# Blocks of two units in one layout: 32 tokens of one sign side by side, for a Fourier mixing and SoLU kernel on one core

## The chip, the core and the metric

The kernel runs on one core of a Trainium2 chip. The core has a matrix engine (TensorE, PE in the profile, whose weight loads are listed apart as PEld), a vector engine (VectorE, DVE), an activation engine (ScalarE, ACT), a general engine (GpSimd, POOL) and a queue engine that issues most transfers (SyncE, SP). SBUF is the on-chip memory of 128 partitions, PSUM the matrix engine's result memory. The metric is the device time of one execution in microseconds (us), as the median of the runs.

## What is computed

Two stages follow each other. `x` is (8, 3136, 256), the weights are (256, 1024) and (1024, 256), all in float32:

```python
X = np.fft.fft(np.fft.fft(x, axis=1), axis=2).real      # (8, 3136, 256)
t = X.reshape(25088, 256)
h = t @ w_in                                            # (25088, 1024)
e = np.exp(h - h.max(-1, keepdims=True))
solu = h * e / (e.sum(-1, keepdims=True) + 1e-9)
mu = solu.mean(-1); var = ((solu - mu) ** 2).mean(-1)
out = ((solu - mu) / np.sqrt(var + 1e-6) * g_ln) @ w_out  # (25088, 256)
```

## The kernel before

**Units.** The sequence length 3136 is split as 49 x 64. The eight batch elements are taken as four pairs, and for each pair and each of 25 frequencies k1 there is one *unit* (class `Unit`, line 251): 128 tokens (2 batch elements x 64 values of k2) in the partitions. By the symmetry of a real transform one unit gives two results, the rows at k1 (sign 0) and the mirrored rows at 49 - k1 (sign 1); only k1 = 0 has one sign. So there are 100 units in a row, 96 of them with two signs.

**One iteration of the main loop** (from line 832) holds work of several units at once, written out by hand in the order in which each engine executes it (`tc.manual_schedule`):

- the *current* unit i: two products with the folded first weights on PE (`up`, line 259; eight matmuls of 512 columns), `even` and `join` on DVE, `expo` on ACT, `product` on DVE (u = h times exp), `square` on ACT, and at the end `turn_both` (line 334), a transpose on DVE in blocks of 32 x 32 from `both` (two signs x 1024 features) into the batch's tile `v`;
- the *previous* unit i - 1: `stats` (line 303), three small ACT instructions that make the variance `v` of each sign with a small term from the exponentials' sums, and `power` (line 313), one GpSimd instruction that raises it to -1/2, the factor `rs`;
- two units together, a *batch* (class `Batch`, line 318): in even iterations `move_blocks` (line 358) issues 16 transfers on SP that carry the 32 x 32 blocks of `v` to `uT`, where features are in the partitions, so that `uT` can be the stationary operand;
- the unit i - 4: `sums` (line 388), four additions or subtractions of 128 x 512 on GpSimd, which make the tiles S from the quarters of `uT`. The first waits for the DVE `product` of unit i - 1[...];
- the unit i - 5: the second product, `Down` (line 403). A unit's two signs of 128 tokens are a 2 x 2 block matrix A, and seven block products (`p1` to `p7`, each eight PE instructions on line 401, since a float32 product takes two) stand for eight, in the manner of Strassen and Winograd. `p1`, `p2` and `p4` have a quarter of `uT` as their stationary operand, the other four have a tile S. ACT (`keep_p`, `keep_x`, `keep_c`) and DVE (`finish`) scale the results with `rs` and join them in `ot`;
- the unit i - 6: `store` (line 475), sign 0 by SP in one transfer of 128 rows, sign 1 by an indirect transfer of GpSimd, whose row numbers are in `idx`.

About half of the iterations also carry a part of the next pair's Fourier stage (lines 109 to 215): loads on SP, additions on GpSimd and DVE, four matmuls on PE, one copy on ACT. The first five units take another way (`turn_whole`, line 341), through transposes on PE. In the last iterations no new units enter, the last batch is moved one unit at a time, and `sums` go to DVE.

**The layouts around the change.** In `v` the element order of a partition is (unit, feature, sign), so a transpose writes every second element:

```python
nc.vector.transpose(out=t.batch.v[:, t.w].rearrange("p f o -> p o f"), in_=t.both)
```

A transfer of `move_blocks` takes 32 partitions, with 16 runs of 64 elements in each (both signs of 32 tokens, alternating), 128 KB. In `uT` the tokens of the two signs therefore alternate as well, and `blocks` (line 379) gives the quarters with a step of two elements (8 bytes) between one stationary column and the next:

```python
uT = t.batch.uT[:, t.w].rearrange("p c i (n s) -> p s c (i n)", s=2)
return [uT[:, s, c : c + KF // 2] for s in range(2) for c in (0, KF // 2)]
```

The tiles S are written without gaps (128 columns in a row). The buffers: two `v`, two `uT`, one S for each unit of a batch, six `ot` for two signs of three units, seven of each small tile.

Of the kernel before, what the change touches and what calls it, by code (L numbers as in the profile page):

```python
# [9 lines left out]
FP32 = mybir.dt.float32  # L10
I32 = mybir.dt.int32
U32 = mybir.dt.uint32
ALU = mybir.AluOpType
# [4 lines left out]
P = 128  # L18


N1, N2 = 49, 64
NK = N1 // 2 + 1
# [4 lines left out]
NC = NH // CH  # L27
# [2 lines left out]


EVEN, ODD = slice(0, 129), slice(129, 256)


@with_exitstack
def kernel(
# [36 lines left out]
    small = ctx.enter_context(tc.tile_pool(name="small", bufs=7))  # L73
# [15 lines left out]
    idx = const.tile([P, NP * (NC + NK - 1)], I32, name="idx")  # L89
# [213 lines left out]
    def stats(t):  # L303

        n = slice(0, len(t.signs))
        es2, v = (small.tile([P, 2], FP32, tag=tag, name=tag) for tag in ("es2", "v"))
        nc.scalar.activation(out=es2[:, n], in_=t.esum[:, n], func=ACT.Square, bias=limits[:, 3:4], scale=1e-3)
        for s in t.signs:
            nc.scalar.activation(out=v[:, s : s + 1], in_=t.ssq[:, s : s + 1], func=ACT.Identity, bias=es2[:, s : s + 1],  # L309
                                 scale=float(FF) ** -3)  # L310
        t.v = v

    def power(t):
        n = slice(0, len(t.signs))
        t.rs = small.tile([P, 2], FP32, tag="rs", name="rs")
        nc.gpsimd.tensor_tensor(out=t.rs[:, n], in0=t.v[:, n], in1=neg_half[:, n], op=ALU.pow)  # L316

    class Batch:


        def __init__(self, by_blocks):
            if by_blocks:
                self.v = fpool.tile([P, 2, FF, 2], FP32, tag="v", name="v32", bufs=2)
            else:
                self.place()

        def place(self):
            self.uT = fpool.tile([P, 2, KF, 4, 64], FP32, tag="uT", name="uT", bufs=2)

    def turn_blocks(t, s):  # L330

        nc.vector.transpose(out=t.batch.v[:, t.w, :, s], in_=t.u[0 if len(t.signs) == 1 else s])

    def turn_both(t):
        if len(t.signs) == 2:
            nc.vector.transpose(out=t.batch.v[:, t.w].rearrange("p f o -> p o f"), in_=t.both)  # L336
        else:
            for s in range(2):
                turn_blocks(t, s)
# [17 lines left out]

    def move_blocks(batch, units, engines=(nc.sync,)):

        v = batch.v[:, units].rearrange("p w (c q n) s -> p q (w c) (n s)", q=4, n=32)  # L360
        uT = batch.uT[:, units].rearrange("p w c i m -> p i (w c) m")
        for i in range(4):
            for q in range(4):
                a, b = slice(32 * i, 32 * i + 32), slice(32 * q, 32 * q + 32)
                engines[i % len(engines)].dma_start(out=uT[b, i], in_=v[a, q])  # L365

# [10 lines left out]
            nc.gpsimd.tensor_tensor(out=Ws[:, j], in0=a, in1=b, op=ALU.subtract)  # L377

    def blocks(t):
        uT = t.batch.uT[:, t.w].rearrange("p c i (n s) -> p s c (i n)", s=2)  # L380
        return [uT[:, s, c : c + KF // 2] for s in range(2) for c in (0, KF // 2)]

# [20 lines left out]
    class Down:  # L403
# [6 lines left out]
        def __init__(self, t, fresh):  # L410
            self.t = t
            self.C11, self.X = (result(i)[:, 0:P] for i in (2, 3))
            self.S = blocks_of(t)
            self.PP = result(1)[:, 0 : 2 * P]
            self.P4, self.P5 = (self.PP[:, i * P : (i + 1) * P] for i in range(2))
            self.A11, self.A12, _, self.A22 = blocks(t)
            t.ot = [fpool.tile([P, D], FP32, tag="ot", name="ot", bufs=6) for _ in range(2)]
            if fresh:

                nc.tensor.matmul(self.X, ident, Wo[:, 0, 0:P], start=True, stop=True, skip_group_check=True)  # L420
# [11 lines left out]
            product7(self.P5, self.S[0], Ws[:, 0])  # L432

        def keep_p(self):
            nc.scalar.mul(out=self.t.ot[1], in_=self.PP, mul=self.t.rs[:, 1:2])  # L435

        def p2(self):
            product7(self.C11, self.A12, Wo[:, KF // 2 :, 0:P])
# [2 lines left out]
            product7(self.X, self.S[1], Ws[:, 1])  # L441

        def keep_x(self):
            nc.scalar.mul(out=self.t.ot[0][:, P:], in_=self.X, mul=self.t.rs[:, 0:1])  # L444

        def keep_c(self):
            nc.scalar.mul(out=self.t.ot[0][:, 0:P], in_=self.C11, mul=self.t.rs[:, 0:1])

        def p3(self):
            product7(self.P5, self.S[3], Wo[:, KF // 2 :, P:])  # L450
# [3 lines left out]

        def finish(self):
            o = self.t.ot[0][:, P:]
            nc.vector.scalar_tensor_tensor(out=o, in0=self.P5, scalar=self.t.rs[:, 0:1], in1=o, op0=ALU.mult, op1=ALU.add)
            o = self.t.ot[1].rearrange("p (i d) -> p i d", i=2)
            nc.vector.scalar_tensor_tensor(out=o, in0=self.X.unsqueeze(1).to_broadcast([P, 2, P]),
                                           scalar=self.t.rs[:, 1:2], in1=o, op0=ALU.mult, op1=ALU.add)  # L460

    def down(t, s, ps=None):

# [4 lines left out]
            nc.tensor.matmul(ps, uT[:, c, :, s], Wo[:, c, :], start=(c == 0), stop=(c == KF - 1))  # L468
        return ps

    def scale(t, s, ps):
        t.ot[s] = fpool.tile([P, D], FP32, tag="ot", name="ot", bufs=6)
        nc.scalar.mul(out=t.ot[s], in_=ps, mul=t.rs[:, s : s + 1])

    def store(t, s):

        if s:
            i = NP * NC + t.p * (NK - 1) + t.k1 - 1
            dma = nc.gpsimd.indirect_dma_start(  # L479
                out=out, out_offset=bass.IndirectOffsetOnAxis(ap=idx[:, i : i + 1], axis=0),  # L480
                in_=t.ot[s], in_offset=None)
        else:
            dma = nc.sync.dma_start(out=out_k[t.p, t.k1], in_=t.ot[s])

        tc.declare_no_dep(dma.ins, group=f"out{1 - s}", reason="other rows of the output")
        tc.add_to_no_dep_group(f"out{s}", dma.ins)

# [183 lines left out]
    with tc.manual_schedule():  # L671
# [77 lines left out]
            keep(first, c, slice(4 * KG, ZR))  # L749
        weights.load_table(1)  # L750
        lag = 5
        whole = 4

        def second_transform(i):
            if i < len(units):
# [4 lines left out]
        def enter(i):  # L760
            cur = units[i]
            if i % 2 == 0:
                batches.append(Batch(i >= whole))
            cur.batch, cur.w = batches[-1], i % 2

        def begin(i):
# [12 lines left out]
        batches = []  # L779
# [52 lines left out]
        for i in range(whole + 1, len(units) + lag + 1):  # L832
# [79 lines left out]
def _tables(B, S, D):  # L912

    import numpy as np

    def cs(num, den):
        a = 2.0 * math.pi * (num % den) / den
        return np.cos(a), np.sin(a)

    n1, k1 = np.arange(N1)[:, None], np.arange(NK)[None, :]  # L920
    c, s = cs(n1 * k1, N1)
    cm, sm = cs((n1 - N1 // 2) * k1, N1)
    zero = np.zeros_like(c)
# [19 lines left out]
    mirror = np.zeros((P, B // 2 * (NC + NK - 1)), np.int32)  # L943
    mirror[:PR, : B // 2 * NC] = load.transpose(1, 0, 2).reshape(PR, -1)
    rows = np.arange(B)[:, None, None] * S + (N1 - np.arange(1, NK)) + N1 * np.arange(N2)[::-1, None]
    mirror[:, B // 2 * NC :] = rows.reshape(B // 2, P, NK - 1).transpose(1, 0, 2).reshape(P, -1)
# [39 lines left out]
```

## Time and profile before

| | |
|---|---|
| runs | 1155.27, 1158.85, 1160.41 us; median 1158.85 us |
| the profiled execution | 1157.6 us, of which the span of the profiled instructions is 1155.8 us |
| granted PE clock | 0.998 of full speed |
| PE | 1109.1 us busy, 96% of the span |
| DVE | 1013.8 us, 88% |
| POOL | 848.0 us, 73% |
| ACT | 758.3 us, 66% |
| transfers | 185.75 MB in 458479 packets, 425750 of them under 512 bytes |

A group's row in the profile reads: line of the kernel, engine, operation, what is written <- what is read, size, count | busy time in us, mean duration in ns of one | idle time of the engine just ahead of it, and what ended that. A row of the timeline reads: start and length in us of a merged stretch, engine, line, operation, count, and in brackets the idle time ahead of it. Matmuls overlap, so the length of a stretch is more than the step from its start to the next one's; the steps between starts are what adds up to the time.

### The profile page before, as it was taken

To read this page: it belongs to the slowest core of one execution; us is meant where nothing else is said; L and a number is where in the kernel's file an instruction comes from. 1 tells how busy PE (TensorE), PEld (TensorE's weight loads), DVE (VectorE), ACT (ScalarE), POOL (GpSimd) and SP (SyncE) were. 2 spreads that over 40 slices of the span, in tenths; PEclk is the share of its full clock that TensorE was granted. 3 is DMA by queue.
4 is the path that set the end of the run, shared out by engine and by line. 5 is a ranking of instruction groups with operands and counts; after the bars stand their busy time and mean duration, and the time that the engine had idled before them with its cause. 6 is when DMAs were issued, how large, how long until landed. Compare 5 with 4: busy or idle time off the path is not lost.

```text
span 1155.8 us, 21664 instructions
## 1 busy us (share of the span) xinstructions
PE 1109.1 (96%) x7026; PEld 888.2 (77%) x7026; DVE 1013.8 (88%) x1440; ACT 758.3 (66%) x1725; POOL 848.0 (73%) x742
## 2 busy tenths in 40 slices
PE   2888999999999999999999999999999999999998
PEld 1555787888887778878887778878778788888887
DVE  7879988888999998888899998888898999898883
ACT  4567667666665766666666766666666676676661
POOL 3035888865898988866689888877499596777764
PEclk9999999999999999999999999999999999999999
DMA  9771798766998779866969697876697675865664
GB/s 238 204 192 39 168 191 195 184 145 145 160 187 160 180 177 184 198 138 143 164 139 204 150 189 171 203 175 141 149 159 146 137 163 122 150 144 111 139 135 111
DMA packets 458479, 185.75 MB, mean 161 GB/s; under 512 B 425750, under 2 KB 440350, under 8 KB 458368
## 3 DMA queue, kind: packets, MB, share of 16 engines
q1 hardware_dynamic: 444608, 146.22, 61.2%
q0 software_dynamic: 13760, 38.16, 12.4%
q8 instruction: 57, 0.93, 0.3%
q14 instruction: 54, 0.44, 0.1%
HBM read 44.78 MB, written 38.80 MB: 72 GB/s over the span
## 4 chain that ended last, share of the span: by engine, by line
PE 81%; DMA 5%; SPq 4%; DVE 4%; issue 2%; POOL 2%; ACT 1%; POOLq 0%; DVEq 0%; ACTq 0%
PE ps_m L401 48%; PE ps_h L264 25%; PE ps_m L208 4%; PE ps_m L236 3%; SPq L365 3%; DMA room<-in_x_dram 2%; DMA uT<-v 1%; DVE h L278 1%; POOL S L394 1%; DMA r<-q 1%; DVE u L293 1%; DMA F<-in_f_tab_dram 1%; SPq L216 1%; PE ps_m L468 1%; PE wps L601 1%
## 5 line engine op out<-in xcount | busy, mean ns | idle before, releaser
L264 PE MATMUL ps_h<-Wi,q 128*128 128x512 f32 x800 | 362.0, 594 | 7.9 <-DVE nmax L278 4.8
L394 POOL TENSOR_TENSOR S<-uT 128x512 f32<-128x512 f32 x186 | 251.1, 1350 | 104.6 <-DMA out_dram<-ot 40.9
L300 ACT ACTIVATE h<-u,usum 128x1024 f32<-128x1024 f32 x196 | 225.2, 1149 | 139.9 <-DVE u L293 139.9
L401 PE MATMUL ps_m<-Ws,S 128*128 128x128 f32 x2304 | 298.7, 276 | 4.3 <-issue 3.0
L401 PEld LDWEIGHTS ps_m<-Ws,S 128*128 128x128 f32 x2304 | 280.8, 192 | 8.8 <-issue 3.3
L264 PEld LDWEIGHTS ps_h<-Wi,q 128*128 128x128 f32 x800 | 144.0, 190 | 155.3 <-issue 139.9
L293 DVE SCALAR_TENSOR_TENSOR u<-h,u 128x1024 f32<-128x1024 f32 x196 | 259.4, 1359 | 0.8 <-ACT u L286 0.7
L286 ACT ACTIVATE u<-h,nmax 128x1024 f32<-128x1024 f32 x196 | 223.6, 1143 | 15.8 <-DVE nmax L278 11.8
L336 DVE STREAM_TRANSPOSE v<-u 128x2048 f32<-128x2048 f32 x93 | 215.5, 2317 | 3.2
L401 PE MATMUL ps_m<-Wo,uT 128*128 128x128 f32 x1536 | 213.1, 282 | 0.0
L401 PEld LDWEIGHTS ps_m<-Wo,uT 128*128 128x128 f32 x1536 | 197.3, 197 | 0.9 <-issue 0.9
L394 POOL TENSOR_TENSOR S<-uT,S 128x512 f32<-128x512 f32 x93 | 133.1, 1431 | 7.3
L278 DVE CUSTOM_DVE_ANT_0 h<-ev,ps_h 128x1024 f32<-128x1024 f32 x100 | 122.1, 1221 | 17.3 <-DVE ev L270 7.9
L479 POOL DMA_INDIRECT out_dram<-ot,idx x96 | 111.2, 1158 | 33.5 <-issue 16.6
L394 POOL TENSOR_TENSOR S<-S,uT 128x512 f32<-128x512 f32 x93 | 126.6, 1362 | 7.3
L278 DVE CUSTOM_DVE_ANT_0 h<-h,ps_h 128x1024 f32<-128x1024 f32 x96 | 117.3, 1221 | 14.2 <-ACT ot L444 0.5
L270 DVE SCALAR_TENSOR_TENSOR ev<-w_mid,r,ps_h 128x1024 f32<-128x1024 f32 x100 | 124.0, 1240 | 4.2 <-DMA r<-q 2.3
L401 PE MATMUL ps_m<-Ws,uT 128*128 128x128 f32 x768 | 106.2, 281 | 0.0
L401 PE MATMUL ps_m<-Wo,S 128*128 128x128 f32 x768 | 102.0, 276 | 0.7 <-ACT ot L435 0.7
L316 POOL TENSOR_TENSOR rs<-v,neg_half 128x2 f32<-128x2 f32 (+1 forms) x100 | 78.2, 782 | 28.4 <-ACT v L309 27.0
L236 PEld LDWEIGHTS ps_m<-T,g 128*128 128x128 f32 x400 | 60.1, 191 | 49.4 <-issue 45.8
L401 PEld LDWEIGHTS ps_m<-Ws,uT 128*128 128x128 f32 x768 | 98.0, 196 | 0.0
(96 smaller groups left out, 1135.5 us busy)
## 6 DMA issues: line engine op xcount, KB each, us to landing
uT<-v SPq DMA_DIRECT2D x752, 128.0 KB
out_dram<-ot SPq DMA_DIRECT2D x100, 128.0 KB
g<-zd POOLq DMA_DIRECT2D x72, 160.0 KB, 5.2
xa<-in_x_dram SPq DMA_DIRECT2D x28, 392.0 KB
zd<-z SPq DMA_DIRECT2D x24, 400.0 KB
raw_in<-in_moe_w_in_dram SPq DMA_DIRECT2D x4, 512.0 KB
raw_out<-in_moe_w_out_dram SPq DMA_DIRECT2D x2, 1024.0 KB
r<-q SPq DMA_DIRECT2D x100, 0.5 KB
```

Of the source, the lines that this page charges most:

```text
L236: nc.tensor.matmul(o, g[:, k, h * P : (h + 1) * P], table, start=(h == 0), stop=True, skip_group_check=True)
L264: nc.tensor.matmul(ps[:, fs], t.q[:, c * P : (c + 1) * P], Wi[:, c, fs], start=True, stop=True)
L270: nc.vector.scalar_tensor_tensor(out=t.ev, in0=w_mid, scalar=t.r, in1=ps, op0=ALU.mult, op1=ALU.add)
L278: nc.vector.tensor_tensor_reduce(out=t.h[s], in0=t.h[0] if s else t.ev, in1=t.odd, scale=1.0 if s else -0.5, scalar=3.0e38, op0=ALU.add, o ...
L286: nc.scalar.activation(out=t.u[s], in_=t.h[s], func=ACT.Exp, bias=t.nmax[:, s : s + 1], scale=-1.0, accum_out=t.esum[:, s : s + 1])
L293: t.last = nc.vector.scalar_tensor_tensor(out=t.u[s], in0=t.h[s], scalar=-1.0, in1=t.u[s], op0=ALU.mult, op1=ALU.mult, accum_out=t.usum[:, ...
L300: nc.scalar.activation(out=t.h[s], in_=t.u[s], func=ACT.Square, bias=t.usum[:, s : s + 1], scale=-float(FF), accum_out=t.ssq[:, s : s + 1])
L316: nc.gpsimd.tensor_tensor(out=t.rs[:, n], in0=t.v[:, n], in1=neg_half[:, n], op=ALU.pow)
L336: nc.vector.transpose(out=t.batch.v[:, t.w].rearrange("p f o -> p o f"), in_=t.both)
L394: i = engine.tensor_tensor(out=S[j], in0=a, in1=b, op=op)
L401: nc.tensor.matmul(o, a[:, c], b[:, c], start=start and c == 0, stop=c == n - 1, skip_group_check=True)
L479: dma = nc.gpsimd.indirect_dma_start(out=out, out_offset=bass.IndirectOffsetOnAxis(ap=idx[:, i : i + 1], axis=0), in_=t.ot[s], in_offset=None)
```

## The change

It concerns the batches whose two units both have two signs, from the third batch to the last but one (`shared`): 44 of the 50 batches, 88 units. For these:

- **Layout of `v`**: (sign and feature group of 32, unit, token of 32). The transpose writes runs of 32 elements.
- **Moves**: still 16 transfers of 32 partitions with 16 runs of 64 elements; a run now holds 32 tokens of one sign of the one unit and 32 of the other.
- **`uT` and the down units**: the token groups 0 and 2 of both units form down unit 0, the groups 1 and 3 down unit 1. A quarter's 128 columns are adjacent.
- **Scaling factors**: a down unit has tokens of two units, so the variances of both are written to `own`, and `mix` (five ACT copies in even iterations, one of 128 partitions and four of 32 partitions from one group of 32 to another) puts them where the down units' tokens are. One `power` of 128 x 4 per batch follows, in place of two of 128 x 2.
- **Stores**: sign 0 of both down units lies in one tile `ot0`; when the second is done, SP stores the batch in four transfers of 32 partitions (64 rows of 1 KB each), in place of one transfer of 128 rows per unit. Sign 1 is stored by GpSimd per down unit as before, with other row numbers. The six `ot` become two `ot0` of two units and three `ot1`.

```diff
+def shared(b, n):
+    return WHOLE // 2 <= b < n - 1 and all(u % NK for u in (2 * b, 2 * b + 1))
...
     def stats(t):
...
+        es2 = small.tile([P, 2], FP32, tag="es2", name="es2")
+        if not t.batch.shared:
+            v = small.tile([P, 2], FP32, tag="v", name="v")
+        else:
+            if t.w == 0:
+                t.batch.own = small.tile([P, 2, 2], FP32, tag="own", name="own", bufs=2)
+            v = t.batch.own[:, t.w]
...
     def power(t):
         n = slice(0, len(t.signs))
+        if t.batch.shared:
+            if t.w:
+                t.batch.power()
+            return
...
+                if self.shared:
+                    self.v = self.v.rearrange("p a f b -> p (a f b)").rearrange("p (g w n) -> p g w n", w=2, n=32)
...
             self.uT = fpool.tile([P, 2, KF, 4, 64], FP32, tag="uT", name="uT", bufs=2)
+            if self.shared:
+                self.uT = self.uT.rearrange("p s c i m -> p (s c) (i m)").rearrange("p b (h m) -> p b h m", h=2)
+
+        def mix(self):
+
+            self.both = small.tile([P, 2, 2], FP32, tag="mix", name="mix", bufs=2)
+            nc.scalar.copy(self.both, self.own)
+            for j in range(4):
+                to, of = slice(32 * j, 32 * j + 32), slice(32 * (j ^ 1), 32 * (j ^ 1) + 32)
+                nc.scalar.copy(self.both[to, 1 - j % 2], self.own[of, j % 2])
+
+        def power(self):
+            self.rs = small.tile([P, 2, 2], FP32, tag="rs2", name="rs2", bufs=3)
+            nc.gpsimd.tensor_tensor(out=self.rs, in0=self.both, in1=neg_half.unsqueeze(1).to_broadcast([P, 2, 2]),
+                                    op=ALU.pow)
...
     def turn_both(t):
-        if len(t.signs) == 2:
+        if t.batch.shared:
+            nc.vector.transpose(out=t.batch.v[:, :, t.w], in_=t.both.rearrange("p s (g n) -> p (s g) n", n=32))
+        elif len(t.signs) == 2:
...
     def move_blocks(batch, units, engines=(nc.sync,)):
+        if batch.shared:
+            v = batch.v.rearrange("p (b q) w n -> p q b (w n)", q=4)
+            parts = batch.uT.rearrange("p b h (a m) -> p b h a m", a=2)
+            uT = [parts[:, :, i % 2, i // 2] for i in range(4)]
...
-                engines[i % len(engines)].dma_start(out=uT[b, i], in_=v[a, q])
+                engines[i % len(engines)].dma_start(out=uT[i][b], in_=v[a, q])
...
     def blocks(t):
+        if t.batch.shared:
+            return [t.batch.uT[:, c : c + KF // 2, t.w] for c in range(0, 2 * KF, KF // 2)]
...
-            t.ot = [fpool.tile([P, D], FP32, tag="ot", name="ot", bufs=6) for _ in range(2)]
+            self.rs = [(t.batch.rs[:, t.w] if t.batch.shared else t.rs)[:, i : i + 1] for i in range(2)]
+            t.ot = [first_out(t), fpool.tile([P, D], FP32, tag="ot1", name="ot1", bufs=3)]
...
+    def first_out(t):
+        if t.w == 0:
+            t.batch.out = fpool.tile([P, 2, D], FP32, tag="ot0", name="ot0", bufs=2)
+        return t.batch.out[:, t.w]
...
     def store(t, s):
...
+        elif t.batch.shared:
+            for j in range(4 if t.w else 0):
+                a, w = divmod(j, 2)
+                rows = out_k[t.p, t.k1 - 1 + w, 64 * a : 64 * a + 64].rearrange("(h n) d -> n h d", h=2)
+                dmas.append(nc.sync.dma_start(out=rows, in_=t.batch.out[32 * j : 32 * j + 32]))
...
             elif old:
                 for s, ps in plain:
                     scale(old, s, ps)
+            if prv and prv.batch.shared and prv.w:
+                prv.batch.mix()
             if cur:
                 for s in cur.signs:
                     join(cur, s)
```

So `mix` stands on ACT between `keep_c` and, where there are any, the small copies of the Fourier stage (line 167), and then the two `expo`.

More of the change, by code (lines that the diff above doesn't have):

```diff
@@ L32 @@
 EVEN, ODD = slice(0, 129), slice(129, 256)
+WHOLE = 4
+def shared(b, n):
+    return WHOLE // 2 <= b < n - 1 and all(u % NK for u in (2 * b, 2 * b + 1))
 @with_exitstack
@@ L88 @@
     neg_half = const.tile([P, 2], FP32, name="neg_half")
-    idx = const.tile([P, NP * (NC + NK - 1)], I32, name="idx")
+    idx = const.tile([P, NP * (NC + NK)], I32, name="idx")
     w_mid = const.tile([P, FF], FP32, name="w_mid")
@@ L305, in stats @@
         n = slice(0, len(t.signs))
-        es2, v = (small.tile([P, 2], FP32, tag=tag, name=tag) for tag in ("es2", "v"))
+        es2 = small.tile([P, 2], FP32, tag="es2", name="es2")
[5 more added lines that the diff above has]
+            v = t.batch.own[:, t.w]
         nc.scalar.activation(out=es2[:, n], in_=t.esum[:, n], func=ACT.Square, bias=limits[:, 3:4], scale=1e-3)
@@ L318, with __init__ @@
     class Batch:
-        def __init__(self, by_blocks):
-            if by_blocks:
+        def __init__(self, b):
+            self.first, self.shared = 2 * b, shared(b, NP * NK // 2)
+            if b >= WHOLE // 2:
                 self.v = fpool.tile([P, 2, FF, 2], FP32, tag="v", name="v32", bufs=2)
+                if self.shared:
+                    self.v = self.v.rearrange("p a f b -> p (a f b)").rearrange("p (g w n) -> p g w n", w=2, n=32)
             else:
@@ L358, in move_blocks @@
     def move_blocks(batch, units, engines=(nc.sync,)):
-        v = batch.v[:, units].rearrange("p w (c q n) s -> p q (w c) (n s)", q=4, n=32)
-        uT = batch.uT[:, units].rearrange("p w c i m -> p i (w c) m")
+        if batch.shared:
+            v = batch.v.rearrange("p (b q) w n -> p q b (w n)", q=4)
+            parts = batch.uT.rearrange("p b h (a m) -> p b h a m", a=2)
+            uT = [parts[:, :, i % 2, i // 2] for i in range(4)]
+        else:
+            v = batch.v[:, units].rearrange("p w (c q n) s -> p q (w c) (n s)", q=4, n=32)
+            uT = [batch.uT[:, units].rearrange("p w c i m -> p i (w c) m")[:, i] for i in range(4)]
         for i in range(4):
@@ L434, in keep_p @@
         def keep_p(self):
-            nc.scalar.mul(out=self.t.ot[1], in_=self.PP, mul=self.t.rs[:, 1:2])
+            nc.scalar.mul(out=self.t.ot[1], in_=self.PP, mul=self.rs[1])
         def p2(self):
@@ L443, in keep_x @@
         def keep_x(self):
-            nc.scalar.mul(out=self.t.ot[0][:, P:], in_=self.X, mul=self.t.rs[:, 0:1])
+            nc.scalar.mul(out=self.t.ot[0][:, P:], in_=self.X, mul=self.rs[0])
         def keep_c(self):
-            nc.scalar.mul(out=self.t.ot[0][:, 0:P], in_=self.C11, mul=self.t.rs[:, 0:1])
+            nc.scalar.mul(out=self.t.ot[0][:, 0:P], in_=self.C11, mul=self.rs[0])
         def p3(self):
@@ L456, in finish @@
             o = self.t.ot[0][:, P:]
-            nc.vector.scalar_tensor_tensor(out=o, in0=self.P5, scalar=self.t.rs[:, 0:1], in1=o, op0=ALU.mult, op1=ALU.add)
+            nc.vector.scalar_tensor_tensor(out=o, in0=self.P5, scalar=self.rs[0], in1=o, op0=ALU.mult, op1=ALU.add)
             o = self.t.ot[1].rearrange("p (i d) -> p i d", i=2)
             nc.vector.scalar_tensor_tensor(out=o, in0=self.X.unsqueeze(1).to_broadcast([P, 2, P]),
-                                           scalar=self.t.rs[:, 1:2], in1=o, op0=ALU.mult, op1=ALU.add)
+                                           scalar=self.rs[1], in1=o, op0=ALU.mult, op1=ALU.add)
     def down(t, s, ps=None):
@@ L469, in down @@
         return ps
+    def first_out(t):
+        if t.w == 0:
+            t.batch.out = fpool.tile([P, 2, D], FP32, tag="ot0", name="ot0", bufs=2)
+        return t.batch.out[:, t.w]
     def scale(t, s, ps):
-        t.ot[s] = fpool.tile([P, D], FP32, tag="ot", name="ot", bufs=6)
+        t.ot[s] = fpool.tile([P, D], FP32, tag="ot1", name="ot1", bufs=3) if s else first_out(t)
         nc.scalar.mul(out=t.ot[s], in_=ps, mul=t.rs[:, s : s + 1])
     def store(t, s):
+        dmas = []
         if s:
-            i = NP * NC + t.p * (NK - 1) + t.k1 - 1
+            i = NP * NC + t.p * NK + t.k1
             dma = nc.gpsimd.indirect_dma_start(
@@ L481, in store @@
                 in_=t.ot[s], in_offset=None)
-        else:
-            dma = nc.sync.dma_start(out=out_k[t.p, t.k1], in_=t.ot[s])
-        tc.declare_no_dep(dma.ins, group=f"out{1 - s}", reason="other rows of the output")
-        tc.add_to_no_dep_group(f"out{s}", dma.ins)
+            dmas.append(dma)
+        elif t.batch.shared:
[3 more added lines that the diff above has]
+                dmas.append(nc.sync.dma_start(out=rows, in_=t.batch.out[32 * j : 32 * j + 32]))
+        else:
+            dmas.append(nc.sync.dma_start(out=out_k[t.p, t.k1], in_=t.ot[s]))
+        for dma in dmas:
+            tc.declare_no_dep(dma.ins, group=f"out{1 - s}", reason="other rows of the output")
+            tc.add_to_no_dep_group(f"out{s}", dma.ins)
     NW = 512
@@ L751 @@
         lag = 5
-        whole = 4
+        whole = WHOLE
         def second_transform(i):
@@ L762, in enter @@
             if i % 2 == 0:
-                batches.append(Batch(i >= whole))
+                batches.append(Batch(i // 2))
             cur.batch, cur.w = batches[-1], i % 2
@@ L942, in _tables @@
     load = row.reshape(-1, PR, 1) * (N2 // CH) + N2 // CH - 1 - np.arange(NC)
-    mirror = np.zeros((P, B // 2 * (NC + NK - 1)), np.int32)
+    mirror = np.zeros((P, B // 2 * (NC + NK)), np.int32)
     mirror[:PR, : B // 2 * NC] = load.transpose(1, 0, 2).reshape(PR, -1)
-    rows = np.arange(B)[:, None, None] * S + (N1 - np.arange(1, NK)) + N1 * np.arange(N2)[::-1, None]
-    mirror[:, B // 2 * NC :] = rows.reshape(B // 2, P, NK - 1).transpose(1, 0, 2).reshape(P, -1)
+    rows = np.arange(B)[:, None, None] * S + (N1 - np.arange(NK)) + N1 * np.arange(N2)[::-1, None]
+    rows = rows.reshape(B // 2, P, NK).transpose(1, 0, 2).reshape(P, -1)
+    for b in range(rows.shape[1] // 2):
+        if shared(b, rows.shape[1] // 2):
+            two = rows[:, 2 * b : 2 * b + 2].reshape(2, 2, 32, 2).transpose(1, 0, 3, 2)
+            rows[:, 2 * b : 2 * b + 2] = two.reshape(2, P).T
+    mirror[:, B // 2 * NC :] = rows
     return {
```

## The prediction

> **What bounds the kernel now.** I read the page's busy shares first, then the timeline of single iterations, the windows, the groups by shape, the waits, and SP's own timeline. The page's first line and its groups on line 401 (the block products):
>
> ```profile
> PE 1109.1 (96%) x7026; PEld 888.2 (77%) x7026; DVE 1013.8 (88%) x1440; ACT 758.3 (66%) x1725; POOL 848.0 (73%) x742
> ...
> L401 PE MATMUL ps_m<-Ws,S 128*128 128x128 f32 x2304 | 298.7, 276 | 4.3 <-issue 3.0
> ...
> L401 PE MATMUL ps_m<-Wo,uT 128*128 128x128 f32 x1536 | 213.1, 282 | 0.0
> ...
> L401 PE MATMUL ps_m<-Ws,uT 128*128 128x128 f32 x768 | 106.2, 281 | 0.0
> L401 PE MATMUL ps_m<-Wo,S 128*128 128x128 f32 x768 | 102.0, 276 | 0.7 <-ACT ot L435 0.7
> ```
>
> PE waits for nearly nothing (4.3, 0 and 0.7 us). The four rows also make a two-by-two table. Whether the moving operand is Wo or Ws makes no difference; with a stationary operand from uT an instruction takes 281 to 282 ns, from S 276. Is that real time or only a modelled end? The timeline of PE over most of one iteration tells:
>
> ```profile
> 508.65 1.11 PE L401 MATMUL ps_m<-Wo,uT 128*128 128x128 f32 x8
> 509.60 1.11 PE L401 MATMUL ps_m<-Ws,uT 128*128 128x128 f32 x8
> 510.54 1.06 PE L401 MATMUL ps_m<-Ws,S 128*128 128x128 f32 x8
> 511.43 1.03 PE L208 MATMUL ps_m<-y,F 98*100 98x258 f32 x4
> 512.30 1.06 PE L401 MATMUL ps_m<-Ws,S 128*128 128x128 f32 x8
> 513.19 1.11 PE L401 MATMUL ps_m<-Wo,uT 128*128 128x128 f32 x8
> 514.13 1.06 PE L401 MATMUL ps_m<-Wo,S 128*128 128x128 f32 x8
> 515.02 1.06 PE L401 MATMUL ps_m<-Ws,S 128*128 128x128 f32 x8
> 515.92 0.59 PE L264 MATMUL ps_h<-Wi,q 128*128 128x512 f32 x1
> ```
>
> No row has a bracket, so PE has no idle time. From start to start a product from uT (p1, p4, p2) takes 0.95, 0.94, 0.94 us, one from S 0.89, 0.89, 0.89, 0.90. Eight instructions differ by 0.05 us: 118 ns apart against 112. The windows, each two iterations (or four in the third, at a change of pairs):
>
> ```profile
> 493.60:515.90 22.30, 22.30 (x146) 18.12 (x145) 19.60 (x30) 15.33 (x38) 16.09 (x15) 1.00 0.61 138
> 1025.40:1046.00 20.60, 20.60 (x139) 16.77 (x138) 18.29 (x25) 14.26 (x33) 14.09 (x13) 1.00 0.59 129
> 286.00:328.00 42.00, 41.48 (x275) 33.56 (x273) 39.41 (x46) 27.85 (x63) 33.23 (x28) 1.00 0.87 163
> ```
>
> Columns: stretch, sum, then PE, PEld, DVE, ACT, POOL. PE fills the first two; DVE leaves 1.35 us free per iteration with a Fourier part (type A, 11.15 us) and 1.16 without (type B, 10.3 us). Only at a change of pairs does PE wait, 0.52 us here, with DVE at 94%; in its fullest iteration there, 306.57 to 317.60, DVE keeps 0.35 us of gaps, which I take as its floor.
>
> [...] additions from uT take 1031 to 1506 ns, `weight_sums` on gapless data 1276. [...] the transpose has 2317 / 2048 = 1.13. [...]
>
> **The change, part by part.**
>
> *Gapless columns for p1, p4, p2.* 24 instructions per down unit, 5 to 6 ns less each: 0.12 to 0.15 us; from the timeline 3 x 0.05 = 0.15. I take 0.145. 88 down units: 12.8 us, all of it on the path where PE is full. Bounds: 0 if the step isn't the cause, 13.4 at most.
>
> *Where PE is not the bound.* Around the three changes of pairs PE waits for DVE, and there a shorter PE waits longer. I count 14 of the 88 down units there: 14 x 0.145 = 2.0 us lost. Bounds 0 and 4.
>
> *mix, on ACT.* Five copies in every even iteration. Nearest rows: the copy of 98x2 on line 167, 185 ns, and the activation of 128x2 on line 307, 293 ns. One of 0.29 and four of 0.19: 1.05 us; bounds 0.93 and 1.47 (all at 0.293). Queued behind it are the two `expo`, and DVE's `product` waits for these. ACT, then DVE, in a type B iteration:
>
> ```profile
> 1044.39 0.37 ACT L447 ACTIVATE ot<-ps_m,rs 128x128 f32<-128x128 f32 x1 [0.57 <-PE ps_m L401]
> 1044.66 1.14 ACT L286 ACTIVATE u<-h,nmax 128x1024 f32<-128x1024 f32 x1
> 1045.70 0.19 ACT L286 ACTIVATION_READ_ACCUMULATOR u<-h,nmax 128x1 f32 x1
> ...
> 1046.58 1.22 DVE L293 SCALAR_TENSOR_TENSOR u<-h,u 128x1024 f32<-128x1024 f32 x1
> ```
>
> The first `expo` is complete at 1045.89, `product` starts at 1046.58: 0.69 us of cover. With mix it starts some 0.4 us later (0.8 at 1.47). That lateness passes through the transpose to `even` and `join`, whose next reader, PE's `up`, comes 2.9 us after `join` ends (514.77 to 517.6 in the type A iteration), and it is made up in the waits of `finish` for PE (0.51 and 0.37 us per iteration). In type A the `product` stands behind the folding, and the cover is 517.25 - 515.92 = 1.33 us. Cost on the path: nothing; ACT itself goes from 66 to about 70% (44 x 1.05 = 46 us).
>
> *power.* Rows: 128x1 579 ns, 128x2 791 ns, so 212 per column; 128x4 about 1.2 us, bounds 0.8 and 1.6. Saved per batch 2 x 0.79 - 1.2 = 0.4 us of POOL. It now waits for mix: in type A it would start at 515.9 instead of 514.48. Behind it stand the indirect store and the next `sums`, which wait for DVE's `product` until 519.78 after 3.35 us of idle time. Hidden. The even/odd shift is harmless, since rs is first read three iterations later.
>
> *Transpose, moves.* Same 2048 columns, 16 transfers, 256-byte runs and 128 KB. [...] 0.
>
> *Stores.* Per batch four transfers for two on SP, plus two issues. SP in type B:
>
> ```profile
> 1024.59 12.92 SPq L365 DMA_DIRECT2D uT<-v  x15
> 1037.61 0.95 SPq L483 DMA_DIRECT2D out_dram<-ot  x1
> 1038.66 0.54 SPq L247 DMA_DIRECT2D r<-q  x1
> 1039.31 0.54 SPq L483 DMA_DIRECT2D out_dram<-ot  x1
> 1040.23 0.53 SPq L247 DMA_DIRECT2D r<-q  x1
> 1044.43 11.59 SPq L365 DMA_DIRECT2D uT<-v  x14
> ```
>
> From 1040.76 to 1044.43 SP waits until p2 frees the buffer: 3.7 us free. Two more issues of 0.5 to 0.95 us fit. The spread r<-q behind them is read two iterations later. The new `ot0` is written again four iterations after its first use, some 11 us after its stores have gone out: no wait. 0.
>
> *The end.* The last batch is not shared. But four stores instead of one stand between its first 16 moves and the other half's (the store at 1133.57, moves until 1140.7): 3 x 0.5 us later on SP. The moves' landing (about 1143.3, at 2.6 to 3.1 us) would come close to DVE's `sums` at 1144.98. I take 0.3 us, bounds 0 and 1.5.
>
> **Sum.** -12.8 + 2.0 + 0.3 = -10.5 us. Span 1155.8 to 1145.3; profiled execution 1157.6 to 1147.1. The median of the runs lies 1.25 us above the profiled execution, so 1148.3.
>
> **Rivals.**
>
> *No gain* (0.10). The 6 ns belong to uT for another reason, such as its place or being written by transfers, and not to the step. For: no group reads a gapless uT. Against: every stationary operand without gaps (S, g, q), in different pools, has 190 to 193 ns per load, and all strided ones 196 to 197. Time: 1158.85 + 0.3, about 1159.
>
> *Half the gain* (0.07). DVE or POOL becomes the bound in more iterations than the 14. Against: DVE's work with its floor of gaps is 11.15 - 1.35 + 0.35 = 10.15 us in type A and 10.3 - 1.16 + 0.35 = 9.49 in B, against PE's new 11.0 and 10.15. Time: about 1153.
>
> *Slower* (0.08). ACT's small copies cost more than these rows[...]. PE feels it in type B once mix exceeds 0.69 us of cover plus DVE's free time of two iterations, 2 x (1.16 - 0.35 - 0.145) = 1.33: at 2.0 us. A pair of iterations is longer than before from 0.69 + 2 x 0.81 = 2.3 us. With some 20 such batches, and 24 of type A that still gain 0.29 us each (7 us together), the kernel is slower from about 2.65 us of mix, 0.53 us per copy. Against: no small ACT row of this trace is over 0.3 us. At 3.0 us: 20 x 0.7 - 7 = +7, about 1166.
>
> *As summed* (0.75): 1145 to 1152 by its bounds and the runs' scatter of 2.5 us to either side.
>
> **How the numbers follow.** 1148.3 is the likeliest case. The low end, 1142, is the full 13.4 us and the scatter, with a little less waiting at the pair changes. The high end, 1156, takes in the half gain; no gain and slower are left out, 0.18 together. A measurement tells 0.5%, 5.8 us, from no change. Faster than 1153.06: 0.75 + half of 0.07, so 0.79. Within: 0.10 + 0.03 = 0.13. Slower: 0.08.
>
> **What would show it.** Right: rows of line 401 from uT at 276 ns, their products 0.89 us from start to start; iterations of 11.00 and 10.14 us with no bracket on PE; mix at 0.9 to 1.5 us; power x44 of about 1.2 us. Wrong: rows from uT still at 281; brackets on PE's `up` that name `join` or `even`; `product` waiting for `expo` by more than 0.8 us; S waiting for uT; SP without free time ahead of its moves.

## The result, and the profile after

The changed kernel takes 1148.8 us (median of 6 runs, 1146.17 to 1150.92); the kernel before, timed beside it, takes 1156.94 us (6 runs, 1155.22 to 1160.41). The ratio is 0.9928, 95% interval 0.9907 to 0.995. The profiled execution took 1150.92 us, its span is 1149.1 us (before: 1157.6 and 1155.8). The forecast of 1148.3 us is met within the scatter, in part by luck: the kernel before, which the forecast took at 1158.85 us, measured 1.9 us less beside it, and the profile shows two terms that the sum didn't have, of opposite sign.

The page's busy line, and the groups of the block products (line 446 now, 401 before):

```profile
PE 1098.1 (96%) x7026; PEld 877.3 (76%) x7026; DVE 993.0 (86%) x1440; ACT 799.3 (70%) x1945; POOL 799.9 (70%) x698
...
L446 PE MATMUL ps_m<-Ws,S 128*128 128x128 f32 x2304 | 297.0, 275 | 0.6 <-POOL xa L142 0.6
...
L446 PE MATMUL ps_m<-Wo,uT 128*128 128x128 f32 x1536 | 205.0, 277 | 0.4 <-DMA out_dram<-ot 0.4
...
L446 PE MATMUL ps_m<-Ws,uT 128*128 128x128 f32 x768 | 103.6, 279 | 0.0
```

The rows from `uT` went from 282 and 281 ns to 277 and 279; their median went from 281 to 275 ns, that of the rows from S. What keeps the means above it are the 8 of 96 units that are not shared and keep the step, and 29 instructions of over 300 ns, 28 of them in two slow stretches to which I come below. PE has 11.0 us less to do. The timeline of PE in an iteration of type A shows it without a mean:

```profile
506.78 1.06 PE L446 MATMUL ps_m<-Wo,uT 128*128 128x128 f32 x8
507.67 1.06 PE L446 MATMUL ps_m<-Ws,uT 128*128 128x128 f32 x8
508.57 1.06 PE L446 MATMUL ps_m<-Ws,S 128*128 128x128 f32 x8
```

A product from `uT` now starts 0.89 to 0.90 us before the next one, as one from S does; before it was 0.94 to 0.95. The windows of two iterations of type A, of two of type B, and of a stretch after the first change of pairs (columns as before: stretch, sum, PE, PEld, DVE, ACT, POOL, granted clock, share and rate of the transfers):

```profile
491.90:513.90 22.00, 22.00 (x147) 17.82 (x145) 19.58 (x30) 16.28 (x42) 15.32 (x14) 1.00 0.70 147
1020.30:1040.50 20.20, 20.20 (x138) 16.37 (x137) 18.16 (x24) 15.00 (x38) 13.12 (x12) 1.00 0.60 130
302.00:306.00 4.00, 3.49 (x19) 3.52 (x20) 3.68 (x5) 1.31 (x5) 3.78 (x6) 0.64 1.28 174
```

In the first two PE is busy throughout, and an iteration takes 11.00 and 10.13 us (11.14 and 10.28 before). The third belongs to what is new. Among the waits of PE (for what, us in total, how often, the longest) there is a line that the kernel before doesn't have:

```profile
PE ps_m L244 <- DMA g<-zd: 8.9, 2, 4.8
```

Line 244 is the first matmul of the Fourier part of the first unit of a new pair; `g` is that pair's input, gathered by four transfers of GpSimd from `zd` in DRAM. At the first and the third change of pairs PE stands still for 4.81 and 4.06 us, and iterations 23 and 73 take 16.81 and 16.06 us instead of 10.29 and 10.28: 6.5 and 5.8 us, 12.3 together. PE at the first of them:

```profile
294.11 3.60 PE L272 MATMUL ps_h<-Wi,q 128*128 128x512 f32 x8
302.51 0.68 PE L244 MATMUL ps_m<-T,g 128*128 128x128 f32 x4 [4.81 <-DMA g<-zd]
```

At the second change (iteration 48) PE has no wait: the first four transfers of `g` are issued at 559.53 there, and PE wants it at 571.05, 11.5 us later. At the first and third it wants it 4.7 and 4.1 us after the first issue.

These two stalls cost more than their waits. Right after each the granted clock is half: 0.50 from 303.09 to 306.49, and again from 842.40 to 845.80; 3.4 us at half speed are 1.7 us of work lost, and 4.81 + 1.7 = 6.5, 4.06 + 1.7 = 5.8.

How the 6.7 us of span come about, from the starts of `up` in both timelines: until unit 9 0.1 us; from unit 9 to unit 99 966.52 - 960.35 = 6.17 us; after that 0.4 us. In the 6.17 us are 84 of the 88 down units (the other four come after unit 99), at 0.147 us each 12.4 us. Iterations 23 and 73 lose 12.6 us against what they would take with the columns' gain. The remaining 6.4 us were gained in single iterations near the changes of pairs (24: 11.03 to 10.13 us, 53: 11.39 to 10.13, and above all 29: 14.59 to 11.10). In iteration 29 the kernel before had a stall of its own: PE waited 2.49 us at 368.42 and had half the clock from 368.98 to 372.38; in the changed kernel it waits 0.58 us and keeps the full clock.

### The profile page after: what moved, and what is told of

Read it like the earlier page. It is cut to its first block, busy times and chain, and to the rows that moved or that the text cites. A ratio compares the mean times of both kernels' runs of the same rounds, so it can differ in the third digit from the quotient of the medians.

```text
span 1149.1 us, 21936 instructions
## 1 busy us (share of the span) xinstructions
PE 1098.1 (96%) x7026; PEld 877.3 (76%) x7026; DVE 993.0 (86%) x1440; ACT 799.3 (70%) x1945; POOL 799.9 (70%) x698
## 3 DMA queue, kind: packets, MB, share of 16 engines
q0 software_dynamic: 13760, 38.16, 12.6%
## 4 chain that ended last, share of the span: by engine, by line
PE 85%; DMA 5%; DVE 4%; issue 2%; ACT 2%; POOL 1%; SPq 1%; POOLq 0%; DVEq 0%
PE ps_m L446 49%; PE ps_h L272 27%; PE ps_m L216 4%; PE ps_m L244 4%; DMA room<-in_x_dram 2%; DMA g<-zd 1%; DVE h L286 1%; DVE u L301 1%; DMA F<-in_f_tab_dram 1%; ACT h L308 1%; PE wps L660 1%; POOL S L439 0%; DVE ev L278 0%; DVE y L150 0%; DMA zd<-z 0%
## 5 line engine op out<-in xcount | busy, mean ns | idle before, releaser
L439 POOL TENSOR_TENSOR S<-uT 128x512 f32<-128x512 f32 x186 | 240.0, 1290 | 97.4 <-DVE u L301 38.8
L301 DVE SCALAR_TENSOR_TENSOR u<-h,u 128x1024 f32<-128x1024 f32 x196 | 239.1, 1256 | 7.2 <-ACT u L294 7.1
L372 DVE STREAM_TRANSPOSE v<-u 128x2048 f32<-128x2048 f32 x88 | 203.4, 2311 | 3.0
L446 PE MATMUL ps_m<-Wo,uT 128*128 128x128 f32 x1536 | 205.0, 277 | 0.4 <-DMA out_dram<-ot 0.4
L446 PEld LDWEIGHTS ps_m<-Wo,uT 128*128 128x128 f32 x1536 | 188.9, 193 | 1.5 <-issue 1.5
L439 POOL TENSOR_TENSOR S<-S,uT 128x512 f32<-128x512 f32 x93 | 120.6, 1297 | 7.3
L439 POOL TENSOR_TENSOR S<-uT,S 128x512 f32<-128x512 f32 x93 | 119.7, 1287 | 7.3
L446 PE MATMUL ps_m<-Ws,uT 128*128 128x128 f32 x768 | 103.6, 279 | 0.0
L216 PE MATMUL ps_m<-y,F 98*100 98x258 f32 (+3 forms) x288 | 72.8, 389 | 23.9 <-DVE y L162 23.9
L446 PEld LDWEIGHTS ps_m<-Ws,uT 128*128 128x128 f32 x768 | 95.6, 195 | 0.0
```

The source lines that it names most:

```text
L216: nc.tensor.matmul(o[..., cs], F[:, 2 * t + h, :], i[..., cs], start=first, stop=True, skip_group_check=True)
L301: t.last = nc.vector.scalar_tensor_tensor(out=t.u[s], in0=t.h[s], scalar=-1.0, in1=t.u[s], op0=ALU.mult, op1=ALU.mult, accum_out=t.usum[:, ...
L372: nc.vector.transpose(out=t.batch.v[:, :, t.w], in_=t.both.rearrange("p s (g n) -> p (s g) n", n=32))
L439: i = engine.tensor_tensor(out=S[j], in0=a, in1=b, op=op)
L446: nc.tensor.matmul(o, a[:, c], b[:, c], start=start and c == 0, stop=c == n - 1, skip_group_check=True)
```

## Experiments

### Which part makes the gain: the columns alone, and all but the columns

The kernel before, with its quarters read as they lie in `uT`, 128 columns in a row (each then holds tokens of both signs, so the products are of other tokens):

```diff
-        uT = t.batch.uT[:, t.w].rearrange("p c i (n s) -> p s c (i n)", s=2)
-        return [uT[:, s, c : c + KF // 2] for s in range(2) for c in (0, KF // 2)]
+        uT = t.batch.uT[:, t.w].rearrange("p c i m -> p c (i m)")
+        return [uT[:, c : c + KF // 2, s * P : (s + 1) * P] for s in range(2) for c in (0, KF // 2)]
```

> The kernel before, with only the reading of uT changed: the quarters' 128 columns are taken as they lie side by side, so they hold both signs of half the tokens and the output is of other tokens than the reference's; every instruction, transfer and count is that of the kernel before. Theory 1 (the step of two elements makes the loads of the stationary operand slow): the rows of the block products from uT fall from 281-282 to 276 ns, the iterations from 11.14 and 10.28 to 11.00 and 10.13 us, and with 92 or more down units the time falls by 10 to 14 us, to about 1145. Rival (uT is slow for where it lies or how it is written): rows and time as before, 1157. On the stall of PE at the first and third change of pairs (4.8 and 4.1 us in the changed kernel): if it comes from the four stores that stand ahead of zd on SP, it is not here, and 1145 or less holds; if it comes from PE's own lead, which lets the block moves start ahead of the g transfers, it is here too and the time is about 1150.

The changed kernel, with every second column for its quarters:

```diff
-            return [t.batch.uT[:, c : c + KF // 2, t.w] for c in range(0, 2 * KF, KF // 2)]
+            uT = t.batch.uT.rearrange("p b h m -> p b (h m)").rearrange("p b (n s) -> p s b n", s=2)
+            return [uT[:, t.w, c : c + KF // 2] for c in range(0, 2 * KF, KF // 2)]
```

> The changed kernel, but a down unit takes every second one of the 256 columns instead of 128 side by side, so its tokens are others than their scaling factors' and the output is not the reference's; all else (moves, mix, power, four stores) is that of the changed kernel. Theory 1: rows from uT back at 281-282 ns, iterations at 11.14 and 10.28 us, 12 to 13 us lost, so 1159 to 1163 if the stalls at the changes of pairs stay, and about 1152 to 1157 if they go. Rival: 1149. On the stalls: with the four stores as their cause they stay, at 2 us or more, since zd is still 2.4 us later on SP than before; with PE's lead as the cause they are gone.

The columns alone: 1149.64 us, ratio 0.9934 [0.9918, 0.995]. All but the columns: 1166.66 us, ratio 1.0091 [1.0068, 1.0114]. The rows from `uT` read 276 and 275 ns in the first, 283 and 282 ns in the second, iterations 11.00 and 10.13 us against 11.14 and 10.28. The first row of each, columns alone and then all but the columns:

```profile
L401 PE MATMUL ps_m<-Wo,uT 128*128 128x128 f32 x1536 | 204.2, 276 | 0.0
```

```profile
L447 PE MATMUL ps_m<-Wo,uT 128*128 128x128 f32 x1536 | 214.0, 283 | 0.9 <-DMA out_dram<-ot 0.9
```

Of what PE reads, only the step between the columns was changed in each, and the rows from S stay at 275 to 276 ns in both, so the step is the cause of the 6 ns; the rival *no gain* falls.

From unit 9 to unit 99 the columns alone gain 9.9 us (956.6), and the rest alone loses 9.4 us (975.9), 8.8 of them in iterations 23 and 73. Both have a wait for `g` at iteration 23, of 1.31 and 2.90 us, the second also 2.40 us at iteration 73. So of the two outcomes that I had expected for the stall neither came whole: each part alone makes a shorter one. The columns alone give part of their gain back at the end: the last stretch takes 51.84 us instead of 48.62, with 2.8 us of PE waiting there for `keep_x`, which I hadn't foreseen. The two parts add up to -0.5 us and together they give -6.2. Part of the difference is that the second kernel is not quite the rest alone: the edit also pairs other columns in GpSimd's two additions from `uT`. Both take 1.5 us there at the median, where the kernel before has one of 1.52 and one of 1.04 and the other two kernels have 1.28 twice; a unit's four additions take 5.92 us on average, against 5.49 before. That may also be why its 1166.66 us lie above the expected range. Beyond that the parts act on each other, as a PE that gets ahead meets other waits; how much that makes was not taken apart.

### Where the stalls come from

The issues of SP around the first change of pairs, kernel before and kernel after, and those of GpSimd for `g`. Before, SP:

```profile
286.93 0.67 SPq L483 DMA_DIRECT2D out_dram<-ot  x1
...
288.87 0.48 SPq L216 DMA_DIRECT2D zd<-z  x1
294.76 14.27 SPq L365 DMA_DIRECT2D uT<-v  x16
```

Before, GpSimd:

```profile
293.52 2.40 POOL L224 DMA_DIRECT2D g<-zd  x4 [8.78 <-DMA zd<-z]
```

After, SP:

```profile
284.60 3.06 SPq L539 DMA_DIRECT2D out_dram<-ot  x4
287.76 0.54 SPq L255 DMA_DIRECT2D r<-q  x1
288.41 0.47 SPq L224 DMA_DIRECT2D zd<-z  x1
...
292.56 16.06 SPq L408 DMA_DIRECT2D uT<-v  x16
```

After, GpSimd:

```profile
293.05 2.40 POOL L232 DMA_DIRECT2D g<-zd  x4 [10.60 <-DMA zd<-z]
```

The last part of `zd` is issued on SP behind the store, and `g` starts 4.6 us after it in both kernels. PE is 2 us earlier by then, and so are the block moves (2.20 us); `zd` is only 0.46 us earlier, because four stores of 3.06 us stand in front of it for one of 0.67. Before, the first of `g` was issued 1.24 us ahead of the first move; now it is 0.49 us behind. Before, `g` had landed when PE wanted it, 4.4 us after its last issue; now its last issue, at 294.88, is followed by 7.6 us until PE goes on. In the two traces of the changed kernel these times are 6.3 to 7.6 us. Where the traces have the landing of the last of the four, it follows the lead that the first issue of `g` has over the first move: 3.5 us after its issue at leads of 2.31 and 2.12 us, 3.7 to 4.3 at 1.76 to 1.24, 5.1 at 0.71, 5.6 to 6.3 at 0.11 to -0.83. So `g` is not only issued late, it also lands more slowly when the moves have begun. The traces show the longer landing, and not how the 16 block moves bring it about.

The theory: the stall needs the stores in front of `zd`. The rival: PE's lead alone makes it. The changed kernel with its batch stores at the end of the iteration, behind `zd`:

```diff
-            if kept:
+            if kept and not kept.batch.shared:
                 store(kept, 0)
...
+            if kept and kept.batch.shared:
+                store(kept, 0)
```

> The changed kernel with SP's four stores of a batch issued at the end of the iteration instead of at its start, so that they stand behind r<-q and zd<-z. If the stores ahead of zd are what lets the block moves overtake the g transfers: zd is issued about 3 us earlier, g lands in 3 to 5 us, PE's waits of 4.8 and 4.1 us for g are gone, and with them 9 to 12 us: 1137 to 1140 us. If PE's lead alone is the cause, zd moves but part of the stall stays: 1143 to 1149.

> The changed kernel with the stores at the end of the iteration, once more. If the stores ahead of zd were the cause of the stalls: again 6 to 9 us under the changed kernel, 1140 to 1143 us, no PE wait for g. If the first result was the luck of some executions: within 3 us of the changed kernel.

It takes 1141.97 us, ratio 0.9883 [0.9862, 0.9903], and in the second set 1143.42 us, 0.9865 [0.9846, 0.9884]. No wait for `g` is left, and unit 9 to unit 99 takes 952.0 and 952.3 us. The changed kernel once more, beside the second:

> The changed kernel once more, for a comparison on the same chip with the three below. 1148 to 1150 us, with PE waits for g of 3 us or more at the first and third change of pairs.

1151.32 us, 0.9934 [0.9917, 0.9952]; stalls of 3.49 and 3.83 us, 959.4 us. The two intervals of this set don't touch: with the stores last the kernel beats both others.

Is it these two places, or the order of the stores everywhere? The stores are moved only in iterations 21 and 71, where the last `zd` part stands behind them:

```diff
-            if kept:
+            if kept and i not in (21, 71):
                 store(kept, 0)
...
+            if kept and i in (21, 71):
+                store(kept, 0)
```

> The changed kernel with the four stores moved to the end of the iteration in two iterations alone, 21 and 71, where zd's last part for the first g of the second and of the fourth pair stands behind them on SP; the other 42 batches store as in the changed kernel. If the stall is made there: PE's waits for g are gone and nearly all of the 8 us of the full move come, 1140 to 1144 us. If the full move gained by SP's order in all iterations: at most 3 us, 1146 to 1150.

1143.04 us, ratio 0.9869 [0.9849, 0.9888], 953.1 us from unit 9 to unit 99, no wait for `g`. SP, and then GpSimd, at the first change of pairs:

```profile
284.96 0.93 SPq L224 DMA_DIRECT2D zd<-z  x1
285.99 2.89 SPq L539 DMA_DIRECT2D out_dram<-ot  x4
...
291.95 14.20 SPq L408 DMA_DIRECT2D uT<-v  x16
```

```profile
290.21 2.42 POOL L232 DMA_DIRECT2D g<-zd  x4 [8.38 <-DMA zd<-z]
```

`g` is 1.74 us ahead of the moves again, although PE keeps its lead. So the stores of two batches of 44 account for the whole difference. The lead of `g` over the moves, and what PE waited, in all traces at both places (the first change of pairs and the third; the kernels without `mix` and with three come further down):

| kernel | place 1: lead of `g`, PE waits | place 2 |
|---|---|---|
| before | 1.24, 0 us | 1.76, 0 us |
| columns alone | 0.71, 1.31 | 1.31, 0 |
| all but the columns | -0.19, 2.90 | 0.11, 2.40 |
| after | -0.49, 4.81 | -1.09, 4.06 |
| after, again | -0.41, 3.49 | -0.42, 3.83 |
| stores last | 2.31, 0 | 2.12, 0 |
| stores last, again | 1.70, 0 | 2.38, 0 |
| two stores last | 1.74, 0 | 1.94, 0 |
| before, stores last | 1.06, 0 | 1.77, 0 |
| after, no `mix` | -0.28, 3.08 | -0.83, 4.09 |
| stores last, no `mix` | 1.70, 0 | 2.48, 0 |
| stores last, three `mix` | 2.32, 0 | 2.68, 0 |

With the columns alone, PE's lead takes 0.5 us from `g`'s (1.24 to 0.71); all but the columns, the four stores among it, takes 1.4 us (to -0.19). Both push, and PE waits at every lead of 0.71 us or less in this table and at none of 1.06 or more.

The same in the kernel before, its store of sign 0 moved to the end of the iteration:

```diff
-            if kept:
-                store(kept, 0)
...
+            if kept:
+                store(kept, 0)
```

> The kernel before with SP's store of sign 0 moved to the end of the iteration in the same way. It has no wait for g, and one store of 0.7 us ahead of zd: if the move helps only by ending that stall, the time stays within 3 us of the kernel before, 1155 to 1160. If late stores help by themselves: 5 us or more less.

1169.63 us, ratio 1.0095 [1.0076, 1.0115]; that it would differ so much I had not expected. ACT's `keep_x` there waits 19.5 us in seven waits for `ot` to be written out (before: 1.9 us in one), PE waits 9.4 us for `keep_x`, and the last stretch takes 55.05 us instead of 48.62. Its `ot` holds three units, and a store that goes out later keeps the buffer longer. So this is no plain control for the order of the stores; what it shows is that late stores everywhere suit the changed kernel, whose `ot0` is written again four iterations after its first use, and not the kernel before.

### Whether mix and the new power cost anything

ACT in a type B iteration of the changed kernel, at `mix`:

```profile
1039.22 0.18 ACT L356 COPY mix<-own 128x4 f32<-128x4 f32 x1
1039.43 0.79 ACT L359 COPY mix<-own 32x2 f32<-32x2 f32 x4
1040.25 1.15 ACT L294 ACTIVATE u<-h,nmax 128x1024 f32<-128x1024 f32 x1
```

1.0 us from 1039.22 to 1040.22. DVE's `product` waits 0.30 us for `expo` in this iteration and 7.1 us in the whole kernel. Without `mix`, so that the factors of half of the tokens are the wrong unit's:

```diff
-            self.both = small.tile([P, 2, 2], FP32, tag="mix", name="mix", bufs=2)
-            nc.scalar.copy(self.both, self.own)
-            for j in range(4):
-                to, of = slice(32 * j, 32 * j + 32), slice(32 * (j ^ 1), 32 * (j ^ 1) + 32)
-                nc.scalar.copy(self.both[to, 1 - j % 2], self.own[of, j % 2])
+            self.both = self.own
```

> The changed kernel without mix: power reads the variances as the units wrote them, so half of the tokens are scaled with another token's factor; five ACT copies per batch are left out, nothing else. If they are hidden, as predicted: the same time within 2 us, 1147 to 1150, although DVE's waits for expo (7.1 us in all) go. If they cost: 4 us or more less.

1153.01 us, ratio 0.9962 [0.9951, 0.9972]: not faster than with `mix`, rather 3 to 4 us slower by the ratios (0.9928 and 0.9934 with `mix`), outside both expected ranges. Its stalls at `g` are 3.08 and 4.09 us, and iteration 29 takes 14.1 us, where GpSimd waits 5.3 us for a transfer, by its place that of `uT` (3.31 in the changed kernel), and PE waits 2.0 us. Over its 22 runs the median granted clock is 0.993, against 0.9955 in the six of the changed kernel; by an estimate from these two, 0.0025 x 1150 us = 2.9 us, the lower clock may make up most of the difference. With the stalls in it a kernel is a poor ground for so small a question; why the clock is lower without `mix` stays open. The same edit on the kernel with the stores last:

> The stores at the end of the iteration and no mix: power reads the variances as the units wrote them, so half of the tokens are scaled with another token's factor. If mix is hidden and the stalls at the changes of pairs are what made its removal look slower: the same time as with mix, within 2 us. If mix costs on the path: 3 us or more less. If its removal itself costs time (power and the indirect stores come earlier on GpSimd): 3 us or more above it.

1145.19 us, ratio 0.989 [0.9871, 0.9908], and 951.9 us from unit 9 to unit 99, beside 952.3 with `mix`. `product`'s waits for `expo` fall from 6.5 to 0.7 us and nothing is gained: `mix` is hidden. (The whole time, 1.8 us above that of 1143.42 with `mix`, is within the scatter of both.)

How much of it can be hidden? The five copies three times over, with the stores last:

```diff
-            nc.scalar.copy(self.both, self.own)
-            for j in range(4):
...
+            for _ in range(3):
+                nc.scalar.copy(self.both, self.own)
+                for j in range(4):
```

> The stores at the end of the iteration and mix done three times over, so 15 copies of 0.2 us, 3.0 us per batch instead of 1.0, the output unchanged. By the prediction's rival the cover in iterations without a Fourier part ends at 2.0 us, so some 20 batches lose about 1.0 us each, and those with one (cover to 3.0 us) lose nothing: 15 to 22 us over the kernel with one mix, about 1160, with PE or DVE waiting for expo there. If DVE and PE have more slack than I worked out: within 5 us of it.

1179.21 us, ratio 1.0186 [1.0167, 1.0205]: 36 us more than with one `mix`, well over the 15 to 22 that I expected. Every second iteration takes longer, by 0.67 us in type A (11.67 us), by up to 0.84 in type B (10.97); the others keep 11.00 and 10.13. From unit 9 to unit 99 the kernel takes 32.1 us more (984.4 against 952.3): about 15 us of them in the 22 regular iterations of type A, about 8 in nine of type B, 7.1 in iterations 31, 55 and 81 alone, and the rest in others near the changes of pairs. Two of its waits, of DVE and of PE:

```profile
DVE u L301 <- ACT u L294: 87.9, 46, 2.4
...
PE ps_m L216 <- ACT q L250: 11.5, 24, 1.8
```

The 15 copies take 3.1 us in the trace. If PE gets everything that exceeds its cover, the cover is 3.1 - 0.84 = 2.3 us in type B, near the 2.0 us that I had worked out, and 3.1 - 0.67 = 2.4 us in type A, where I had let every pair keep its gain at 3.0 us. The second line names the way in type A: the copy of `q` on line 250 is queued on ACT behind `mix`, and PE's Fourier matmuls (line 216) wait for it, 24 times, nearly all of them in the longer iterations of type A. The matmuls stand 0.43 us as a rule, the weight loads ahead of them 0.62 us, which is nearly the 0.67. This is read from the waits, and was not tried alone.

## Why the prediction was right, and where it was not

- **The gapless columns** were right in mechanism and size: 0.94 to 0.89 us per product, 11.00 and 10.13 us per iteration for 11.00 and 10.14 forecast, and the two experiments on the step show the cause.
- **Where PE is not the bound**: the sign was wrong. I took 2.0 us off; outside the two stalls these iterations gained 6.4 us beyond the columns instead. Most of that goes with the stalls; as I read it, the other engines catch up while PE stands. Without stalls (stores last, and two stores last) 1.1 to 2.1 us of it are left; iterations 24 to 29 take 67.1 us before, 61.8 in the changed kernel and 64.4 to 64.9 in these. The mean of DVE's `product` shows the same: 1359 ns before, 1256 in the changed kernel, 1304 and 1310 with the stores last and two stores last, but 1374 with the columns alone and 1377 with the rest alone. In the kernel before, the 154 products with no GpSimd addition of `sums` beside them took 1.21 to 1.24 us; 33 of the 196 took over 1.3 us, every one of them beside such an addition, and 23 of these over 2.0; after only 7, with the stores last 20. So it takes both parts to bring the number down. Which of the saved `power`, the even additions or the earlier PE moves GpSimd out of DVE's way was not tried alone.
- **mix**: 1.0 us for 1.05 forecast, hidden as argued, `product` 0.30 us later for 0.4. The threshold in the rival *slower* was wrong for type A: I had followed the lateness through `product` and `join`, and not through the other instructions behind `mix` in ACT's queue, the copy of `q` among them.
- **power**: 1.04 us for 1.2, hidden. **Transpose**: 2311 ns for 2317, no change; the 0 for it had been an estimate. **The end**: 48.25 us for 48.62, a gain of 0.4 where four down units should bring 0.6; the lost 0.2 us are near the 0.3 that I took off, but a second profile of the changed kernel has 47.66 us, so one trace can't tell.
- **Stores: the step that failed.** "From 1040.76 to 1044.43 SP waits until p2 frees the buffer: 3.7 us free." That is true of the iteration that I read, of type B away from a change of pairs. In iterations 21 and 71 `zd`, and through it `g`, stands behind the stores, and I priced only the reader of `r<-q`. I asked what is queued behind the stores in one iteration, and not in the two of 100 where the answer differs. That the stall comes from these two stores is shown by moving them alone: 6.3 to 7.3 us from unit 9 to unit 99 (959.4 and 960.4 against 953.1), less than the stalls' 12.3 us, since after a stall the next iterations make up some of it, as said above.
- **The total** is right with the help of both errors and of the base: the forecast gain was 10.5 us, the measured one 1156.94 - 1148.8 = 8.1 us, and the forecast time is met so closely because the kernel before was 1.9 us faster beside it than the 1158.85 us from which I started. The stalls that were not foreseen cost 12.6 us in their two iterations; against that stand the 6.4 us gained near the changes of pairs and the 2.0 us that I had taken off there. With the two stores moved the ratio is 0.9869, 1157.13 to 1143.04, 14.1 us: without the stalls the change is worth more than I forecast.

## What to carry to other kernels

Price a step's queue neighbours in the iteration where the rarest of them stands behind it, not in the steady one: a transfer that is free in 42 of 44 places may carry the whole cost in the other two. A faster bounding engine brings its own transfers forward too; where two transfers were ordered by 1.2 us of luck, write out by hand which goes first. And follow the lateness of an added instruction through everything behind it in its engine's queue, not only through the consumer that one has in mind.

## What was not expected of the hardware

- A stationary operand with 8 bytes from column to column costs 118 ns per instruction of 128 columns where an unbroken one costs 112 (starts 0.94 to 0.95 and 0.89 to 0.90 us apart for eight of them); 24 instructions in each of 88 units make 12.7 us.
- GpSimd's additions of 128x512 with both operands from `uT` depend on how the two lie to each other. At a step of 8 bytes the median is 1.52 us when both are of the same sign (A21 + A22), so in the same one of the two interleaved places, and 1.04 us when they are of different signs (A11 - A21); without gaps both take 1.28 us. In the kernel with all but the columns both operands of either addition lie in the same place, and both take 1.5 us. One addition of each kind together takes 2.56 us with the step and without it; two operands in the same place take 0.24 us more with it, two in different places 0.24 us less. (The means on the pages, 1350 and 1290 ns, don't show it: additions beside a DVE `product` are in them, and with the columns alone the mean is 1355.)
- After PE has stood for 4.8 us, the granted clock is 0.64 over the next window of 4 us (the third line of the windows above), 0.50 over the 3.4 us from 303.09, and a product there takes 1.65 to 1.7 us from start to start instead of 0.89. In the traces of the kernels before and after, the gaps of PE of over 1 us between unit 9 and unit 99 are of 2.49, 4.81 and 4.06 us; 0.55, 0.57 and 0.99 us after their ends, at 368.97, 303.08 and 842.39, begin 3.41 us at 0.50, and there is no other stretch of that kind; the next longest gap of either, 0.88 us, is followed by none. With all but the columns the block products after the gap of 2.90 us at `g` start 1.71 and then 1.16 us apart; after gaps of 1.31 us (columns alone) and 1.43 us (three `mix`) they start 0.89 to 0.97 us apart. Not every long gap has such a stretch: of the 14 of 1.77 us or more in all twelve traces, 12 have one within 1.5 us of their end, and two others, of 3.00 and 2.90 us, have none. The traces show the clock that was granted, and not what sets it.
- The four stores of a batch (32 partitions, 64 rows of 1 KB each) occupy SP for 2.7 us at the median, 2.0 to 3.3 us in all; a store of 128 rows in the kernel before takes 0.70 us at the median, 0.33 to 3.0. A store of 32 partitions moves half as many rows and takes 0.44 us at the median, so smaller transfers are cheaper one by one, but four cost more than the two that they replace.
